# Clustered attention and a gated feed-forward: reordering conversion work and maxima among five queues, and laying the first row shifts by matrix products

## The chip, the cores and the metric

The kernel runs on one core of one Trainium2 chip. The metric is the device time of one execution in microseconds (us). The five engines have queues of their own, and each works through its queue in order: TensorE (PE in the profile; its weight loads are PEld), VectorE (DVE), ScalarE (ACT), GpSimd (POOL) and SyncE (SP), which here only issues transfers.

## The reference

```python
# q, k, v: (4, 8, 768, 64); centroids: (8, 16, 64); w_in: (512, 2048); w_out: (2048, 512)
q_assign = argmax(einsum('bhsd,hcd->bhsc', q_n, c_n), -1)     # rows normalised
k_assign = argmax(einsum('bhsd,hcd->bhsc', k_n, c_n), -1)
mask   = q_assign[:, :, :, None] == k_assign[:, :, None, :]
scores = where(mask, scale * q @ k.T, -1e9)
scores = scores - max(scores, -1)
attn   = exp(scores) / (sum(exp(scores), -1) + 1e-9)
x      = (attn @ v) laid out as (4 * 768, 512)
h      = x @ w_in
out    = (h * erf(log(1 + exp(h)))) @ w_out
```

Each query attends only to the keys of its own cluster, and the attention output goes through a feed-forward with the activation h·erf(softplus(h)). The feed-forward weights arrive in double precision.

## The kernel before, in words

**Pairs and units.** Two heads are worked on together as a pair: four batches of four pairs. A pair has 12 units: two halves of the queries (384 each) times six blocks of 128 keys. A unit `u` has these stages:

- `products`: scores q·k of both heads, in float32 (`sc<-qT,kT` in the profile);
- the rest of `scores`: a bf16 product that adds the mask (`sc<-qm,km`), and on ScalarE the exponential into `pr`;
- `accumulate`: GpSimd adds up the exponentials (`acc`);
- `attend`: the product with v (`av`);
- `divide`, once per half: the denominators (`psum`, `inv`, `den`) and the result into `xT`.

**The mask, the shift and the rows.** The mask is built into the operands `km` and `qm`: their lower rows hold, per cluster, a one-hot code (or minus a large number), so that their product adds a large negative number where the clusters differ. One more row of each head (partition `SH` = 32 for head 0, 96 for head 1) holds in `qm` the negated shift of each query and in `km` ones, so the same product also subtracts it. `route(p)` finds the clusters: it transposes q and k on VectorE, casts them into `qm` and `km` (`vectors`), multiplies with the centroids (`psim`), finds the best (`sims`, `mx`, `hot`, `hotT`), and `choose` picks the first winner by a product (`wonq`, `wonk`) and copies it into the operands. These are the mask copies: four on ScalarE into `km`, two on ScalarE and two on VectorE into `qm`. Pairs of later batches use `choose_later`, which works without `won`.

**The maxima.** `shift(p)` computes the shift: for each of six blocks of queries, two halves of the keys and two heads a product `sm<-km,qm` and, on VectorE, a maximum over 384 (`nmx<-sm`). After three blocks the shifts of one half (`nm`) are complete, and `turn(p, h)` brings them from a column per block into the row: a transposition on TensorE (`pn`), a copy on ScalarE (`nmT`), and six transfers of 128 elements (`qm<-nmT`).

**The weights.** `convert()` turns the double-precision weights into float32 in 32 steps of 128x512 with integer tricks. A step `n` has: two ScalarE operations that split the words (`split`), one VectorE maximum, one ScalarE operation for the signs (`signs`), a transfer for a later step (`fetch`), then, in a second call, a VectorE shift and a GpSimd addition, and the next step's `split`. Every `yield` ends a call; `prepare(n)` makes `n` calls. In the profile all of these have `w_out` or `a_s` as their ScalarE output, since the raw words are staged there.

**The order.** The first batch's attention has its order written out by hand. Two units form a period; a pair has six, counted by `r` = 0, 2, 4, 6, 8, 10. For each, `plan` gives five numbers: how many steps of the pair's own `aside` (routing, then maxima) go ahead of the scores, how many of the next pair's; how many of each go behind them; and how many conversion calls follow. `turn(p, 1)` stands ahead of r=4, `turn(p+1, 0)` ahead of r=10. With `keep_in_program_order` the engines keep the order of the program here; near the end of the batch (`in_order[0] = False`) the scheduler may reorder. From the second batch on, the feed-forward's products (`hp`, `po`) fill the gaps between units, and the rest of the conversion is spread out.

**Buffers.** PSUM has two tiles for scores (`ps_s`) and four for everything else (`ps_x`): `sm`, `psim`, `won`, `pn`, `psum`, `av`, `hp`, `po`. An `av` tile stays in use over a half.

The plan before, one line per three periods, as (own ahead, next ahead, own behind, next behind, conversion calls):

```python
(1, 0, 1, 1, 0), (1, 0, 0, 2, 0), (0, 0, 0, 1, 4),
(0, 1, 0, 2, 2), (0, 1, 0, 2, 0), (0, 1, 0, 2, 2),
```

In the next pair's `aside`, the first call is the transposition and the cast of q, the second `psim` and the cast of k, the third the choice of winners, the fourth the mask copies; each call after that is two maxima.

Of the kernel before, what the change touches and what calls it, by code (L numbers as in the profile page):

```python
# [8 lines left out]
F32 = mybir.dt.float32  # L9
# [9 lines left out]
P = 128  # L19
B, H, S, D = 4, 8, 768, 64  # L20
# [4 lines left out]
HW = S // 2  # L25
HJ = NJ // 2
# [14 lines left out]
SH = 2 * C  # L41
# [27 lines left out]
def kernel(  # L69
# [10 lines left out]
    nc = tc.nc  # L80

    in_order = [True]
    te, ve, ae, ge = (
        InOrder(tc, e, in_order) for e in (nc.tensor, nc.vector, nc.scalar, nc.gpsimd)
    )

    def pool(name, bufs, **kw):
        return ctx.enter_context(tc.tile_pool(name=name, bufs=bufs, **kw))
# [13 lines left out]
    ps_x = pool("ps_x", 4, space=PSUM)  # L102

    ident = const.tile([P, P], F32, name="ident")
    identb = const.tile([P, P], BF16, name="identb")
# [20 lines left out]
    pairs = {}  # L126
# [43 lines left out]
    for base, pattern, sign, op, fill in (  # L170
# [5 lines left out]
            out=first, in_=first, compare_op=op, fill=fill, base=base, pattern=pattern,  # L176
# [9 lines left out]
    w_steps = []  # L186
# [11 lines left out]
        return actp.tile([P, NFT // 2, TB], F32, name="a_s")  # L198

    steps = {}  # L200

    def fetch(done):

        for n in range(max(done + 1, 0), min(done + 5, len(w_steps))):
            at = places[n]
            if n in steps or (at < 4 and at in places[done + 1 : n]) or (at == 4 and n > done + 2):
                continue
            t = half_tile() if at == 4 else w_out[:, 4 * at : 4 * (at + 1)]
            t = t.rearrange("p f t -> p (f t)").bitcast(U32)
            nc.sync.dma_start(out=t[:, 0 : 2 * LC], in_=w_steps[n][1])  # L210
            raw = t[:, 0 : 2 * LC].rearrange("p (n w) -> p n w", w=2)
            steps[n] = raw[:, :, 1], raw[:, :, 0], t[:, 2 * LC : 3 * LC], t[:, 3 * LC : 4 * LC]

    def split(n):

        if n < len(w_steps):
            hi, lo, m, x = steps[n]
            ae.activation(out=x.bitcast(F32), in_=hi.bitcast(F32), func=ACT.Abs, scale=UP)
            ae.activation(out=m.bitcast(I32), in_=lo, func=ACT.Copy, scale=2.0**-29)

    def signs(n):

        hi, _, m, _ = steps[n]

        ae.activation(
            out=m.bitcast(I16)[:, 1 : 2 * LC : 2], in_=hi.bitcast(F32), func=ACT.Prelu,
            scale=2.0**-25, alpha=2.0**90,
        )

    def convert():  # L230

        split(0)
        for n in range(len(w_steps)):
            _, _, m, x = steps[n]
            w = w_steps[n][0]
            xf = x.bitcast(F32)
            ve.tensor_scalar(out=xf, in0=xf, scalar1=2.0, scalar2=None, op0=ALU.max)
            signs(n)

            fetch(n - 2 if n < n_w_in else n - 1)  # L240
            yield
            ve.tensor_scalar(
                out=w.bitcast(U32), in0=x, scalar1=3, scalar2=None, op0=ALU.logical_shift_left
            )

            ge.tensor_tensor(out=w.bitcast(I32), in0=w.bitcast(I32), in1=m.bitcast(I32), op=ALU.add)
            converted[0] = n + 1
            split(n + 1)
            yield

    load_qk(0)
# [18 lines left out]
    for it in range(2):  # L270
# [4 lines left out]
            out=twice, in0=ss, scalar=inv, in1=norm, op0=ALU.mult, op1=ALU.add  # L275
# [3 lines left out]
            out=norm, in0=twice, scalar1=0.5, scalar2=(1e-6 if it else 0.0),  # L279
# [124 lines left out]
    def shift(p):  # L404


        st = pairs[p]
        nmx = maxima[p % 2]
        load(p, "v", v, vp)
        for h in range(2):  # L410
            ts = slice(h * HJ, (h + 1) * HJ)
            for t in range(h * HJ, (h + 1) * HJ):
                for half in range(2):
                    for e in range(2):
                        sm = ps_x.tile([P, HW], F32, name="sm", tag="x")
                        te.matmul(
                            sm, lhsT=st["qm"][:, e, t * P : (t + 1) * P],
                            rhs=st["km"][:, e, half * HW : (half + 1) * HW], start=True, stop=True,
                        )
                        ve.tensor_reduce(  # L420
                            out=nmx[:, e, t, half : half + 1], in_=sm, axis=AX.X, op=ALU.max, negate=True
                        )
                    if (t, half) != ((h + 1) * HJ - 1, 1):
                        yield
            nm = small.tile([P, 2, HJ], BF16, name="nm")
            ve.tensor_reduce(out=nm, in_=nmx[:, :, ts], axis=AX.X, op=ALU.min)
            st["nm", h] = nm
            if p >= HP:
                yield
                turn(p, h)  # L430
            yield

    def turn(p, h):

        st = pairs[p]
        pn = ps_x.tile([2 * HJ, P], BF16, name="pn", tag="x")
        te.transpose(out=pn, in_=st["nm", h].rearrange("p e t -> p (e t)"), identity=identb)
        nmT = small.tile([2 * HJ, P], BF16, name="nmT")
        ae.copy(out=nmT, in_=pn)
        for e in range(2):  # L440
            r = e * D + SH
            for t in range(HJ):

                queue = nc.scalar if (p, h, e) == (0, 0, 1) else nc.sync
                queue.dma_start(
                    out=st["qm"][r : r + 1, e, h * HW + t * P : h * HW + (t + 1) * P],
                    in_=nmT[e * HJ + t : e * HJ + t + 1],
                )

# [7 lines left out]
    def products(u):  # L459
        p, half, j = units[u]  # L460
        st = pairs[p]
        sc = sc_of[u] = ps_s.tile([P, 2, 512], F32, name="sc", tag="s")
        for e in range(2):
            r = slice(e * D, (e + 1) * D)
            te.matmul(
                sc[:, e, 0:HW], lhsT=st["kT"][r, j * P : (j + 1) * P],
                rhs=st["qT"][r, half * HW : (half + 1) * HW], start=True, stop=False,
            )
# [182 lines left out]


    conv = convert()

    def prepare(n):
        for _ in range(n):
            next(conv, None)
# [3 lines left out]
    def aside(p):  # L661
# [3 lines left out]


    plan = (
        (1, 0, 1, 1, 0), (1, 0, 0, 2, 0), (0, 0, 0, 1, 4),
        (0, 1, 0, 2, 2), (0, 1, 0, 2, 0), (0, 1, 0, 2, 2),
    )  # L670
    ready = {0: aside(0)}
    part = iter(())
# [1 line left out]
    def advance(p, n):  # L674
        for _ in range(n):
            next(ready[p])
# [5 lines left out]
    for e in range(2):  # L682
        ve.tensor_copy(
            out=ccT[e * D : (e + 1) * D, :, e * C : (e + 1) * C],
            in_=pct[e * D : (e + 1) * D].rearrange("d (r e c) -> d r e c", e=2, c=C)[:, :, e],
# [11 lines left out]
    for e in range(2):  # L697
        ve.reduce_sum(
            out=own[:, e : e + 1],
            in_=ident.rearrange("p (g x c) -> p x g c", x=2, c=C)[:, e], axis=AX.XY,  # L700
        )
    advance(0, 1)
    products(0)
    products(1)
    advance(0, 2)
    prepare(2)
    advance(0, NJ + 1)
    turn(0, 0)
    prepare(1)
    advance(0, HJ - 1)  # L710
    for slot in range(0, 2 * NJ * HP, 2):
        p, r = divmod(slot, 2 * NJ)
# [4 lines left out]
        if r == 4:  # L717
            turn(p, 1)
        elif r == 10 and p + 1 < HP:
            turn(p + 1, 0)  # L720
# [34 lines left out]
    for u in range(2 * NJ * HP, len(units), 2):  # L755
        p, half, j = units[u]
# [59 lines left out]
```

The softmax here doesn't subtract the row's maximum and nothing guards it: scores larger than these inputs give would overflow.

## Time and profile before

| | |
|---|---|
| time, median of 3 (lowest to highest) | 1215.78 us (1215.23 to 1217.73) |
| span of the profiled run | 1211.9 us |
| TensorE busy | 1150.3 us (95%) |
| VectorE, ScalarE, GpSimd busy | 43%, 47%, 38% |
| mean granted TensorE clock | 0.977 |

The span is the time of the profiled execution on the core. Nearly all lines of the kernel carry the line number L60 in the profile, the helper through which instructions are issued, so groups are told apart by the tiles that they write and read: `sm<-km,qm` is the maxima's product, `nmx<-sm` the maximum itself. A wait is written as the engine that waited, an arrow, and the engine and tile that released it. Busy shares are averages over stages that differ: the first batch's attention takes roughly the first 175 us, and the feed-forward fills the rest.

### The profile page before, as it was taken

The page shows a single profiled execution, that of the slowest core. Times are in us where ns is not written, and L with a number is a line of the kernel's source. Part 1 is how long each engine was busy: PE and PEld are TensorE (multiplying, and loading weights), DVE is VectorE, ACT ScalarE, POOL GpSimd, SP SyncE. Part 2 cuts the span into 40 slices and gives each one's busy share as a digit, 9 for nine tenths or more (in the row PEclk, how much of TensorE's full clock was granted, in tenths as well). Part 3 has the DMA queues.
Part 4 walks back from the last instruction along what each step waited for, and adds up shares of the span by engine and source line. Part 5 has one row for each costly group of instructions (what it writes and reads, how often), then busy time and mean ns, then how long its engine had stood idle before and what let it go on. Part 6 is the DMA issues. An engine that isn't in the chain of part 4 may idle for free.

```text
span 1211.9 us, 13334 instructions
## 1 busy us (share of the span) xinstructions
PE 1150.3 (95%) x4905; PEld 622.7 (51%) x4905; DVE 518.1 (43%) x976; ACT 571.0 (47%) x680; POOL 460.5 (38%) x466
## 2 busy tenths in 40 slices
PE   4888879899999989999999999999999999999998
PEld 1223337554454545465465455556456456576663
DVE  6576783764444444344263345335354112111121
ACT  4676586677343535173454355165264163122222
POOL 2665764555332433144244243344143343031200
PEclk7799889999999999999999999999999999999999
DMA  7543432212020201020200202001000000000000
GB/s 136 126 94 73 84 112 63 86 48 47 2 48 10 48 8 33 9 36 14 36 22 1 48 10 40 9 17 32 10 23 1 10 9 1 18 1 18 1 17 18
DMA packets 140753, 42.95 MB, mean 35 GB/s; under 512 B 133520, under 2 KB 133520, under 8 KB 140688
## 3 DMA queue, kind: packets, MB, share of 16 engines
q1 hardware_dynamic: 137456, 41.70, 15.7%
q10 hardware_dynamic: 3232, 0.39, 0.3%
q8 instruction: 39, 0.64, 0.2%
q14 instruction: 26, 0.21, 0.1%
HBM read 35.68 MB, written 6.29 MB: 35 GB/s over the span
## 4 chain that ended last, share of the span: by engine, by line
PE 79%; DVE 7%; issue 6%; ACT 5%; DMA 2%; POOL 1%; ACTq 0%; SPq 0%; DVEq 0%; POOLq 0%
PE hp L60 25%; PE po L60 25%; PE sc L60 13%; PE av L60 9%; PE sm L60 4%; DVE nmx L60 2%; PE psum L60 1%; PE psim L60 1%; ACT km L60 1%; ACT L60 1%; DVE w_out L60 1%; DVE den L60 1%; DMA a_s<-in_moe_w_out_dram 1%; ACT inv L60 1%; ACT w_out L60 1%
## 5 line engine op out<-in xcount | busy, mean ns | idle before, releaser
L60 PE MATMUL hp<-xT,w_in 128*128 128x256 f32 x1536 | 381.4, 385 | 2.8 <-DVE xT L60 2.0
L60 PE MATMUL po<-w_out,g 128*128 128x512 f32 x768 | 368.0, 597 | 0.6 <-DVE den L60 0.6
L60 PEld LDWEIGHTS hp<-xT,w_in 128*128 128x128 f32 x1536 | 285.9, 191 | 119.9 <-issue 81.0
L60 POOL TENSOR_TENSOR acc<-acc,pr 128x384 f32<-128x384 f32 x256 | 238.2, 961 | 283.4 <-ACT pr L60 283.3
L60 DVE TENSOR_REDUCE nmx<-sm 128x1 f32<-128x384 f32 x384 | 195.7, 551 | 149.6 <-PE sm L60 148.7
L60 ACT ACT_TABLE_LOAD x110 | 141.1, 1283 | 234.6 <-DVE g L60 128.9
L60 ACT ACTIVATE pr<-sc 128x768 f32<-128x768 f32 x192 | 145.0, 806 | 157.2 <-PE sc L60 156.7
L60 PEld LDWEIGHTS po<-w_out,g 128*128 128x128 f32 x768 | 142.2, 190 | 105.9 <-issue 93.0
L60 POOL TENSOR_TENSOR g<-a_s,g 128x512 f32<-128x512 f32 x88 | 110.5, 1287 | 214.7 <-ACT a_s L60 214.7
L60 PE MATMUL sc<-qT,kT 64*128 64x384 f32 x768 | 178.3, 526 | 4.8 <-ACT pr L60 4.7
L60 DVE COPY g<-hp 128x512 f32<-128x512 f32 x96 | 66.0, 687 | 265.8 <-PE hp L60 265.6
L60 PE MATMUL av<-pr,in_v 128*64 128x386 f32 x768 | 141.2, 509 | 0.6 <-DVE nmx L60 0.6
L60 PE MATMUL sm<-km,qm 128*128 128x384 bf16 x384 | 109.8, 347 | 31.0 <-DVE nmx L60 20.2
L60 PEld LDWEIGHTS sc<-qT,kT 64*128 64x128 f32 x768 | 73.8, 192 | 80.5 <-issue 46.7
L60 POOL TENSOR_TENSOR acc<-pr,pr 128x384 f32<-128x384 f32 x64 | 63.5, 1013 | 104.9 <-ACT pr L60 104.9
L60 PEld LDWEIGHTS av<-pr,in_v 128*64 128x64 f32 x768 | 52.2, 140 | 79.5 <-issue 68.8
L60 PEld LDWEIGHTS <-qm 128*128 128x128 bf16 x384 | 35.2, 99 | 105.4 <-issue 80.8
L60 DVE SCALAR_TENSOR_TENSOR den<-psum,inv 128x384 f32<-128x384 f32 x32 | 17.7, 554 | 124.5 <-ACT inv L60 124.1
L60 ACT ACTIVATE a_s<-a_s 128x2048 f32<-128x2048 f32 (+3 forms) x48 | 62.0, 1309 | 15.1 <-DMA a_s<-in_moe_w_out_dram 14.6
L60 ACT ACTIVATE a_s<-g 128x2048 f32<-128x2048 f32 x24 | 45.9, 1910 | 39.2 <-DVE g L60 39.1
L60 PE MATMUL sc<-qm,km 64*128 64x384 bf16 x384 | 56.2, 328 | 4.3 <-DMA qm<-nmT 4.3
L60 ACT ACTIVATE w_out<-w_out 128x512 f32<-128x512 f32 (+2 forms) x72 | 47.0, 702 | 8.9 <-DMA w_out<-in_moe_w_out_dram 4.7
(72 smaller groups left out, 544.4 us busy)
## 6 DMA issues: line engine op xcount, KB each, us to landing
w_out<-in_moe_w_in_dram SPq DMA_DIRECT2D x16, 512.0 KB, 4.5
in_q<-in_q_dram SPq DMA_DIRECT2D x64, 96.0 KB, 3.1
in_v<-in_v_dram SPq DMA_DIRECT2D x32, 192.0 KB, 2.9
out_dram<-osb SPq DMA_DIRECT2D x24, 256.0 KB, 2.0
in_k<-in_k_dram SPq DMA_DIRECT2D x60, 96.0 KB, 3.4
w_out<-in_moe_w_out_dram SPq DMA_DIRECT2D x8, 512.0 KB, 3.7
a_s<-in_moe_w_out_dram SPq DMA_DIRECT2D x8, 512.0 KB, 3.3
qm<-nmT SPq DMA_DIRECT2D x189, 0.2 KB, 1.7
```

Of the source, the lines that this page charges most:

```text
L60: ins = getattr(self.engine, name)(*args, **kw)
```

## The change

The change has three parts. First, the split of step `n+1` is queued in the first call of step `n`, right after `signs(n)`, instead of at the end of its second call; `split(upto)` splits everything up to a step that has been fetched, and remembers in `cut` what it did. The splits of steps 0 and 1 are queued by hand at the start. It is meant to keep VectorE's conversion operations from waiting for splits that stand behind other ScalarE work. Second, the plan moves maxima away from the period whose ScalarE queue holds the mask copies: no maxima ahead of the scores of r=6, four ahead of r=8 and r=0; and it spreads the conversion calls: one each in r=0 and r=2, two instead of four in r=4. Third, the first shifts of all are laid into their row by six products with one column of `nm` each (`turn_first`), whose outputs start at the row's own partition, and by one copy per head, instead of a transposition, a copy and six transfers.

```diff
-    def split(n):
-
-        if n < len(w_steps):
+    def split(upto):
+
+        for n in range(len(cut), upto + 1):
+            if n not in steps:
+                return
+            cut.append(n)
             hi, lo, m, x = steps[n]
             ae.activation(out=x.bitcast(F32), in_=hi.bitcast(F32), func=ACT.Abs, scale=UP)
             ae.activation(out=m.bitcast(I32), in_=lo, func=ACT.Copy, scale=2.0**-29)
...
     def convert():
 
-        split(0)
         for n in range(len(w_steps)):
+            split(n)
...
             signs(n)
+            split(n + 1)
...
             converted[0] = n + 1
-            split(n + 1)
             yield
...
+    def turn_first():
+
+        st = pairs[0]
+        pn = ps_x.tile([P, HJ, P], F32, name="pnr", tag="x")
+        for e in range(2):
+            r = slice(e * D + SH, e * D + SH + 1)
+            for t in range(HJ):
+                te.matmul(pn[r, t], lhsT=st["nm", 0][:, e, t : t + 1], rhs=identb, start=True, stop=True)
+            (ae.copy, ve.tensor_copy)[e](
+                out=st["qm"][r, e, 0:HW], in_=pn[r].rearrange("p t n -> p (t n)")
+            )
...
     plan = (
-        (1, 0, 1, 1, 0), (1, 0, 0, 2, 0), (0, 0, 0, 1, 4),
-        (0, 1, 0, 2, 2), (0, 1, 0, 2, 0), (0, 1, 0, 2, 2),
+        (2, 0, 0, 1, 1), (1, 0, 0, 2, 1), (0, 0, 0, 1, 2),
+        (0, 0, 0, 2, 2), (0, 2, 0, 2, 0), (0, 1, 0, 2, 2),
     )
...
     advance(0, 1)
+    split(0)
     products(0)
     products(1)
     advance(0, 2)
+    split(1)
     prepare(2)
     advance(0, NJ + 1)
-    turn(0, 0)
+    turn_first()
     prepare(1)
```

More of the change, by code (lines that the diff above doesn't have):

```diff
@@ L200 @@
     steps = {}
+    cut = []
     def fetch(done):
@@ L442, in turn @@
             for t in range(HJ):
-                queue = nc.scalar if (p, h, e) == (0, 0, 1) else nc.sync
-                queue.dma_start(
+                nc.sync.dma_start(
                     out=st["qm"][r : r + 1, e, h * HW + t * P : h * HW + (t + 1) * P],
```

## The prediction

> **What bounds the kernel now.** I read the page first, then the table by windows, the chain that ended last, and the timeline of one pair of heads.
>
> ```profile
> span 1211.9 us, 13334 instructions
> ...
> PE   4888879899999989999999999999999999999998
> ...
> PEclk7799889999999999999999999999999999999999
> ```
> The page: TensorE is busy nearly throughout, except in the first six slices of 30.3 us, where its clock is also low.
>
> ```profile
> 60.00:90.00 30.00, 25.09 (x138) 9.08 (x134) 22.51 (x42) 23.52 (x36) 18.06 (x19) 0.93 0.42 92
> ...
> 120.00:150.00 30.00, 25.85 (x134) 8.91 (x130) 21.24 (x42) 17.51 (x28) 20.78 (x22) 0.89 0.35 78
> ...
> 300.00:400.00 100.00, 99.21 (x426) 48.06 (x430) 43.78 (x87) 37.91 (x51) 35.18 (x39) 1.00 0.13 26
> ```
> The windows (busy time of PE, PEld, DVE, ACT, POOL, then clock): from 300 us TensorE is 99% busy at full clock, so a microsecond won early is kept. In the first batch's attention (30 to 175 us) it idles 4 to 5 us in 30, and no other engine is full either. That is a queue waiting on a queue, and the chain shows which:
>
> ```profile
> 115.15 0.81 ACT pr L60
> ...
> 115.98 0.57 ACT km L60
> ...
> 118.93 0.57 ACT qm L60
> ...
> 119.53 1.25 ACT w_out L60 x2
> ...
> 120.80 1.29 ACT w_out L60 x2
> ...
> 122.11 1.10 DVE w_out L60
> 123.21 0.48 DVE nmx L60
> ...
> 123.73 1.41 PE sm L60 x3
> 125.14 2.77 PE av L60 x8
> ```
> Read from top: exponential, six mask copies, conversion splits, a conversion op on VectorE, a maximum, and only then TensorE. It stands in each of the first three pairs at the same place, period r=4 to r=6; TensorE does little from 79.2 to 86.3 us in the second pair. Then it pays again:
>
> ```profile
> 84.00:85.00 1.00, 0.00 (x0) 0.00 (x0) 0.35 (x1) 1.00 (x3) 0.81 (x1) 1.00 0.00 0
> ...
> 86.00:87.00 1.00, 0.73 (x2) 0.21 (x2) 1.00 (x3) 0.99 (x2) 1.00 (x2) 0.50 0.78 295
> ...
> 91.00:92.00 1.00, 1.00 (x5) 0.57 (x6) 0.95 (x2) 0.00 (x0) 1.00 (x2) 0.50 0.71 262
> ...
> 93.00:94.00 1.00, 1.00 (x10) 0.30 (x6) 0.00 (x0) 0.44 (x1) 0.00 (x0) 1.00 0.00 0
> ```
> The clock (third figure from the end) is halved for some 6.8 us after the gap; a period's av products take 2.77 us there against 1.45 elsewhere in the chain.
>
> At the start, the same chain, earlier:
>
> ```profile
> 25.88 0.18 DVE nm L60
> ...
> 29.10 1.66 DMA qm<-nmT
> ...
> 30.90 0.83 PE sc L60 x4
> ```
> The first shifts are known at 26.06 and reach the scores at 30.90, through a transposition, a copy and six small transfers.
>
> **What the Trainium skill says.** (1) "TensorE: Matmul & The Clock Gate", What's actually happening: the clock halves after an idle window of about 3.4 us and comes back after a busy one; the windows run freely. The trace agrees on the grid (drops at about 44.8 and 85.8 us are twelve windows apart) but a window need not be empty: the one ending at 44.8 was 1.6 of 3.4 us busy. (2) "DMA: Bandwidth & Descriptors", Anatomy of one DMA: about 2.0 us fixed, mostly the write's receipt (stated for another issuing path); the qm<-nmT transfers here have 1.7 us median. (3) The TensorE page, What picks the tile position: a product's output may start at partition 0, 32, 64 or 96. That is what lets the shifts land in rows 32 and 96; no product of the kernel before has a one-row output.
>
> **The change, part by part.** I call S the start of a period's score products on TensorE. In the second pair S is 66.05, 70.17, 75.16, 81.17, 91.13, 98.57, 103.50 for r = 0, 2, 4, 6, 8, 10 and the next 0: lengths 4.12, 4.99, 6.01, 9.96, 7.44, 4.93, together 37.45 us. The same work at full clock is about 28 us (six periods of 1.81 sc + 1.45 av; 24 maxima products at 0.215; psum 1.6, psim 0.8, won and pn 0.6).
>
> *a. First shifts by products, first split earlier.* ScalarE waits 2.19 us for wonk before its mask copies; the first split (2 x 0.67 = 1.33) fits there and costs nothing. Then VectorE's first conversion op need not wait until 19.39: it follows the qm copies at 16.4, its two ops end at 17.3, and the twelve maxima, 0.48 each, end at 23.1 instead of 25.86: 2.7 us. The shifts: six products of 128 columns (between 0.1 and 0.27 each, the pn product being 0.27; I take 0.2, so 1.2) and two copies of 1x384. Unknown: at least the 0.25 of the nmT copy, at most the 0.57 of a 384-column copy; I take 0.5, side by side on two engines. About 1.8 us replaces 4.84. The rows are thus ready near 25. But the program now puts eight maxima products ahead of the first scores (six before), and VectorE needs 0.48 for each: scores near 27.9 instead of 30.9. **3.0 us**, with two maxima already done that formerly came after.
>
> *b. Splits a period sooner.* Nothing is removed: each conversion step keeps three ScalarE ops (2.05 to 2.08 together), two VectorE (0.43 each) and one GpSimd (1.27). Only the order changes. In r=4, VectorE's conversion op finds its split done in r=2, so no split behind the mask copies holds the maxima queue: the 2.58 + 1.10 us of conversion in the chain above leave it.
>
> *c. Two of r=4's four conversion calls go to r=0 and r=2.* r=0 gets VectorE 0.43 and GpSimd 1.27, hidden: VectorE waits for sm there. r=2 gets ScalarE 2.05 and VectorE 0.43. That isn't hidden: ScalarE's r=2 is 1.51 (pr) + 1.12 (inv) + 1.67 (km cast) + 0.25 (nmT) = 4.55 of 4.99. The conversion is queued ahead of nmT, so in r=4 nmT ends 2.1 later, at S4+3.45, and pr starts at S4+3.5 instead of S4+1.82. Behind nmT stand six transfers whose rows the r=6 scores read: at 0.61 per issue (76.55, 3.66 for six) plus 1.7 the last lands at S4+8.25; at the 6.1 us of the fourth pair (151.34 to 157.42), at S4+9.5. This is the change's new wait: TensorE has nothing from about S4+5.8 until then, bar one score in between.
>
> *d. Maxima away from the mask copies.* r=6 no longer begins with two maxima that wait for km; its scores' first products go at S4+4.4 instead of S4+6.0. The eight maxima of r=6 and of r=8's head then run at VectorE's pace.
>
> Sum from S4 to S8: ScalarE: pr to 5.0, km copies 7.4, qm 8.5, conversion 10.6, r=6's pr 12.1. TensorE: scores' masks end at 8.7 to 9.6, four maxima 1, av 1.45, four maxima 1.9 (VectorE: 4 x 0.49, 0.86 of conversion, 4 x 0.49): S8 = S4+12.8 to 13.7 at full clock. The new gap is long enough to halve the clock where the window falls badly; then av takes 2.8 and maxima 0.47 each: S8 = S4+16.0. I take S4+14.5, against 15.97: -1.5. r=8 then runs at full clock, about 6.9 for 7.44: -0.5. The four maxima ahead of r=0 cost +0.7 there and give 0.4 back: +0.3. **-1.7 a pair, three pairs -5.1.** The fourth pair has a routing of its own; its km copies now come behind r=6's pr, which waits for the same transfers, but six ScalarE ops fewer stand before them: **0**, from -1 to +2.
>
> *e. Afterwards* the order of work is the same and TensorE the bound: carried over in full.
>
> Sum: 3.0 + 5.1 = 8.1: **1207.7 us**.
>
> **The rivals.**
> - *All gain, no new gap*: the transfers land early and the clock holds: S8 at S4+12.8: 3.2 + 0.6 - 0.3 = 3.5 a pair, 10.5 + 3.0: 1202.3. For: TensorE's floor of 28 us leaves room for nine. Against: ScalarE's overfull r=2.
> - *The new wait takes the old one's place*: the shift transfers and a halved clock give S8 at S4+16: 0.2 a pair, 0.6 + 3.0: 1212.2. For: 1.6 us busy in a window was already too little. Against: with six issues at 0.61 the gap is only 2.4.
> - *Given back later*: the second batch's start hangs on the remaining conversions (waits on a_s transfers of 3.15 to 3.35 us near 227 to 249 us), half of 8.1 lost: 1211.7. For: those waits are on the chain. Against: they are relative, started by the work before.
> - *Slower*: r=2's 2.05 us lie on the path in full in all four pairs, 8.2 against the start's 3.0: 1221. For: ScalarE is in order, pr and nmT are behind it. Against: 3.7 us of conversion leave the chain in the same pair.
>
> **How the numbers follow.** Forecast 0.45, no new gap 0.20, new wait 0.22, given back 0.07, slower 0.06. The range 1202.0 to 1212.8 takes in the first four. The bound of 0.2% lies at 1213.3: the forecast and the full gain are faster, of the two cases near 1212 about two thirds: 0.85. Same 0.09, slower 0.06.
>
> **What would show it.** In the trace after: first scores near 28 us (a); no conversion between qm copies and maxima in the chain (b); nmT of r=4 behind three w_out ops, and a wait of sc on qm<-nmT in r=6 of each pair (c); r=4 to r=8 near 14.5 us (d); equal lengths after 300 us (e). Wrong would be: no such wait on the transfers (then it's nearer 1202), a pair of 37 us or more, or a first score after 29.5.

## The result and the profile after

| | before | after |
|---|---|---|
| median, first measurement | 1216.6 us (4 runs, 1215.23 to 1217.73) | 1201.19 us (4 runs, 1197.01 to 1205.72) |
| profiled execution, span | 1211.9 us | 1204.0 us |
| TensorE busy | 1150.3 us | 1148.0 us |

The ratio is 0.9875, with a 95% interval of 0.9837 to 0.9912: faster by about 15 us. The four times after spread over 8.7 us, the four before over 2.5; in later measurements of 11 or 12 runs, the kernel before spread over 4.6, 7.0 and 8.4 us, so a wide spread is not peculiar to the changed kernel. The profiled execution is the slowest of the four, so the two traces differ by 7.9 us only.

The page after, rows as before the change:

```profile
span 1204.0 us, 13336 instructions
...
PE   4888899899999989999999999999999999999998
...
PEclk8899999999999999999999999999999999999999
```

and the windows, with the same columns as in the prediction (busy PE, PEld, DVE, ACT, POOL, clock):

```profile
60.00:90.00 30.00, 25.70 (x147) 9.51 (x146) 21.72 (x45) 24.09 (x38) 23.53 (x24) 1.00 0.46 111
...
120.00:150.00 30.00, 24.73 (x144) 9.14 (x141) 24.27 (x46) 18.76 (x29) 19.28 (x20) 0.98 0.30 56
...
300.00:400.00 100.00, 99.43 (x438) 48.05 (x437) 43.25 (x85) 42.31 (x55) 29.96 (x32) 1.00 0.15 29
```

TensorE is hardly busier than before in the same 30 us, but its clock is 1.00 and 0.98 there where it was 0.93 and 0.89, and the work comes earlier. What stands at the old place now shows in the chain that ended last (start, length, what), in the third pair:

```profile
106.42 0.56 ACT w_out L60
...
107.60 0.66 ACT w_out L60
108.26 0.14 ACT nmT L60
108.45 0.32 PE wonk L60
...
110.21 1.34 PE sc L60 x7
111.55 1.68 DMA qm<-nmT
...
113.36 0.48 PE sc L60 x3
...
115.14 2.77 PE av L60 x8
```

The splits behind the mask copies, and the maximum behind the splits, are gone from this chain. In their place stand conversion, the copy nmT behind it, the transfers behind that, and the scores behind the transfers. The second product of r=4, wonk, waits for nmT too, by 1.1 us. In this pair the clock falls again (av at 2.77 us). The second pair has the same chain and keeps its clock:

```profile
77.87 1.59 DMA qm<-nmT
...
79.60 0.48 PE sc L60 x3
...
81.32 1.45 PE av L60 x8
```

The start after:

```profile
23.93 0.18 DVE nm L60
...
24.16 0.34 PE pnr L60 x3
24.52 0.48 ACT qm L60
...
25.04 0.34 PE pnr L60 x3
...
25.48 0.56 DVE qm L60
...
29.01 0.77 PE sc L60 x4
```

Eleven further runs were made. The table gives their medians and, from each trace, the time from S4 to S8 in the second and third pair (S: start of a period's first score products), and the start of ScalarE's first activation over a whole half tile (`a_s<-g`), the first gate, a mark at the end of the first batch. The runs were made on several chips; each ratio is to runs of the kernel before on the same chip, whose medians lie between 1214.2 and 1216.6 us.

| kernel | median us | ratio to before, 95% | S4 to S8 | first gate |
|---|---|---|---|---|
| before | 1216.6 | 1 | 15.97, 15.97 | 191.2 |
| after | 1201.19 | 0.9875 (0.9837 to 0.9912) | 12.44, 14.05 | 179.7 |
| e1_after | 1204.21 | 0.9904 (0.9882 to 0.9927) | 13.98, 12.52 | 180.2 |
| e11_after | 1202.62 | 0.9895 (0.9872 to 0.9918) | 12.44, 12.51 | 179.5 |
| e2_start | 1209.93 | 0.9962 (0.9948 to 0.9976) | 15.97, 15.99 | 188.1 |
| e3_no_start | 1204.91 | 0.9910 (0.9893 to 0.9926) | 12.35, 14.05 | 181.8 |
| e4_split_only | 1207.67 | 0.9943 (0.9924 to 0.9963) | 12.91, 12.92 | 182.7 |
| e5_plan_only | 1208.08 | 0.9945 (0.9925 to 0.9966) | 13.66, 13.86 | 181.2 |
| e8_warm | 1202.73 | 0.9899 (0.9884 to 0.9915) | 12.44, 12.53 | 177.6 |
| e6_turn_first | 1198.20 | 0.9862 (0.9843 to 0.9880) | 11.13, 11.13 | 174.3 |
| e7_r8 | 1196.70 | 0.9850 (0.9831 to 0.9869) | 11.24, 11.31 | 171.9 |
| e9_early | 1197.38 | 0.9852 (0.9826 to 0.9878) | 11.24, 11.23 | 173.5 |
| e10_prod | 1203.59 | 0.9906 (0.9886 to 0.9925) | 11.23, 11.23 | 178.8 |

The changed kernel's first four runs were probably a favourable draw: the two later medians, of six runs each, are 1204.21 and 1202.62, though the three intervals overlap. In all three of its traces the first gate comes 11.1 to 11.8 us sooner than in the trace before; that is the part that repeats.

### The profile page after: what moved, and what is told of

The parts are those of the page before. It is cut to its first block, busy times and chain, and to the rows that moved or that the text cites. A ratio compares the mean times of both kernels' runs of the same rounds, so it can differ in the third digit from the quotient of the medians.

```text
span 1204.0 us, 13336 instructions
## 1 busy us (share of the span) xinstructions
PE 1148.0 (95%) x4910; PEld 621.8 (52%) x4910; DVE 513.9 (43%) x977; ACT 569.7 (47%) x680; POOL 461.0 (38%) x466
## 4 chain that ended last, share of the span: by engine, by line
PE 79%; issue 7%; DVE 5%; ACT 4%; DMA 4%; POOL 1%; SPq 0%; ACTq 0%; DVEq 0%; POOLq 0%
PE hp L60 26%; PE po L60 25%; PE sc L60 13%; PE av L60 8%; PE sm L60 4%; DVE nmx L60 2%; PE psum L60 1%; PE psim L60 1%; ACT L60 1%; DMA a_s<-in_moe_w_out_dram 1%; DMA in_k<-in_k_dram 1%; DMA w_out<-in_moe_w_out_dram 1%; DVE den L60 1%; ACT inv L60 1%; DMA qm<-nmT 1%
## 5 line engine op out<-in xcount | busy, mean ns | idle before, releaser
L60 PE MATMUL sm<-km,qm 128*128 128x384 bf16 x384 | 105.8, 341 | 19.5 <-DVE nmx L60 13.0
L60 ACT COPY nmT<-pn 6x128 bf16<-6x128 bf16 x31 | 7.7, 248 | 87.6 <-PE pn L60 87.6
```

The costliest lines, as they stand in the source:

```text
L60: ins = getattr(self.engine, name)(*args, **kw)
```

## The experiments

**e1_after and e8_warm: what spreads the times.** e1_after is the changed kernel unaltered. e8_warm puts eight products whose result nobody reads where TensorE waits for the transfers:

```diff
+        if us[0] < 2 * NJ * HP and us[0] % (2 * NJ) == NJ:
+            idle = ps_x.tile([P, HW], F32, name="idle", tag="x")
+            for _ in range(8):
+                te.matmul(idle, lhsT=identb, rhs=pairs[units[us[0]][0]]["km"][:, 0, 0:HW], start=True, stop=True)
```

> The changed kernel once more, for other draws of its time and another trace. Theory 'clock': the change leaves two short waits of TensorE around r=4 and r=6 (about 1.1 us on won, 1.5 us on the shift transfers), and the free-running activity window decides whether they halve the clock; so the times spread over 1195 to 1206, each follows its own granted clock (about 1.2 us for each 0.001), and the median is 1198 to 1202. Rival 'queues': the order of the queues alone sets the time; the spread has to come from the later batches and does not follow the clock, and S4 to S8 is the same in every trace (12.4 us in the second pair, 14.0 in the third).

> The changed kernel with eight extra products of 128x384 that nobody reads, between the first products of r=6 and its mask products, where TensorE waits for the shift transfers; about 1.7 us of work in a wait of 1.5. Theory 'clock': the clock stays at 1.00 through r=6 and r=8 of all pairs, S4 to S8 is 12.4 to 12.8 us in the second and the third pair alike, the spread narrows and the median falls to 1195 to 1199. Rival 'queues': the extra products stand ahead of the mask products in an in-order queue and cost up to 0.3 us a pair: 1200 to 1204, with the same spread.

In e1_after it is the second pair that loses its clock and the third that keeps it, the other way round than in the first trace. The second pair in the first trace, then in e1_after (the clock is the third figure from the end):

```profile
80.00:85.00 5.00, 4.35 (x23) 1.79 (x24) 4.55 (x10) 4.81 (x8) 4.12 (x5) 1.00 0.99 275
80.00:85.00 5.00, 4.62 (x17) 1.43 (x18) 2.62 (x6) 4.95 (x9) 4.13 (x5) 0.66 0.95 262
```

The program is the same, so the order of the queues alone does not decide between 12.4 and 14.0 us. The traces show what goes with it. The shortest stretches at half clock last 3.4 us. The two falls in the first trace, at 43.2 and 114.9 us, lie 21 times 3.41 us apart. If time is cut into windows of 3.41 us, counted from the first fall after 40 us, every change of the clock up to about 165 us falls on an edge of a window, in the trace before and in all three of the changed kernel. A window at full clock in which TensorE was busy for 1.70 us or less was followed by half clock every time (twelve cases), one with 1.85 us or more never. In the first trace of the changed kernel, the windows with the wait for the transfers and those after them are, for the second and for the third pair:

```profile
77.35:80.77 3.42, 1.91 (x13) 0.59 (x10) 0.38 (x1) 3.35 (x6) 3.42 (x4) 1.00 0.29 65
80.77:84.18 3.41, 2.86 (x15) 1.04 (x16) 3.34 (x9) 3.39 (x7) 2.53 (x4) 1.00 1.01 284
...
111.49:114.90 3.41, 1.58 (x10) 0.47 (x8) 0.75 (x2) 3.33 (x7) 3.41 (x5) 1.00 0.47 106
114.90:118.31 3.41, 3.41 (x11) 1.06 (x11) 1.87 (x5) 3.38 (x6) 2.47 (x3) 0.50 0.88 300
```

The waits for the transfers are alike (1.42 and 1.50 us), but in the third pair a wait of 0.32 us for the maxima falls into the same window, and in the second pair most of it comes after the edge. The edges lie differently in each execution: the first fall comes at 43.2, 43.9 and 44.6 us in the three traces of the changed kernel. In the first pair the clock fell in all three, and S4 to S8 took 14.3 to 14.5 us. This was read from the traces afterwards; no experiment moved the edges.

e8_warm, with the wait filled, kept the clock at 1.00 through its first three pairs, as theory 'clock' said, but not in the fourth: S4 to S8 took 12.2 us in the first pair, 12.44 and 12.53 in the next two, and its first gate came 2.6 us before e1_after's. Nothing of this reached the end: its median of 1202.73 lies in the rival's range, and its ratio overlaps that of e1_after, whose own median of 1204.21 lies outside the 1198 to 1202 of theory 'clock'. From 200 us, e8_warm's windows show where the lead goes:

```profile
200.00:205.00 5.00, 2.40 (x13) 1.10 (x15) 2.23 (x4) 4.94 (x5) 1.56 (x2) 0.91 0.00 0
205.00:210.00 5.00, 5.00 (x16) 2.49 (x9) 4.29 (x8) 3.51 (x6) 5.00 (x5) 0.50 0.08 13
210.00:215.00 5.00, 5.00 (x13) 3.30 (x12) 2.48 (x5) 2.01 (x3) 2.21 (x2) 0.57 0.35 116
```

and e1_after's the same place:

```profile
200.00:205.00 5.00, 4.05 (x22) 2.24 (x21) 0.82 (x2) 4.94 (x5) 0.00 (x0) 1.00 0.35 79
205.00:210.00 5.00, 3.27 (x14) 1.49 (x14) 3.48 (x6) 4.97 (x7) 3.98 (x4) 0.77 0.02 3
210.00:215.00 5.00, 5.00 (x20) 3.39 (x19) 5.00 (x10) 1.40 (x3) 3.77 (x4) 0.89 0.35 105
```

There TensorE waits while ScalarE is full (4.94 of 5 us) with the gates and table loads. In these 15 us it is idle about as long in both (2.6 and 2.7 us), but e8_warm then runs at half clock for some 10.2 us, worked out from the clock in its windows, and e1_after for 3.4. Its third gate activation starts at 246.5 us, e1_after's at 246.2: the whole lead is lost. Later the clock also separates the first trace of the changed kernel from e1_after. Up to the fifth activation they agree (393.36 and 393.40 us); the sixth starts at 448.21 in the first and 445.06 in e1_after. The slower one's windows between:

```profile
400.00:410.00 10.00, 8.89 (x35) 4.76 (x34) 5.25 (x9) 6.66 (x8) 6.67 (x6) 0.92 0.09 31
410.00:420.00 10.00, 10.00 (x42) 6.04 (x43) 5.05 (x10) 2.18 (x4) 5.68 (x7) 0.91 0.01 3
...
430.00:440.00 10.00, 7.33 (x32) 3.72 (x30) 0.69 (x1) 5.07 (x6) 3.59 (x4) 0.83 0.00 0
```

e1_after has 1.00 in all three, with TensorE busy for the same time to within 0.1 us: 3.2 us for the clock alone, and this is all of the difference between the two spans (1204.0 and 1200.8). One more part of the expectation fell: the mean granted clock does not order the runs (0.989 went with 1200.8 and with 1204.7). Only these differences between traces are shown; that the whole spread of 9 us comes from the clock is not, and the kernel before spreads nearly as far on one chip.

**e2_start and e3_no_start: the start alone, and all but the start.** e2 adds `turn_first` and the early `split(0)` to the kernel before; e3 takes both (and `split(1)`) from the changed kernel. Of e3's edit, the lines for the first shifts:

```diff
-    turn_first()
+    turn(0, 0)
```

> Part a alone on the kernel before: the first shifts by products, and the first split queued ahead of the first mask copies. If the start's gain is kept to the end, 2.5 to 4 us less than before (1212.5 to 1214). Rival: the first pair's loads and the conversions set its pace anyway, and the earlier scores wait in r=2 instead: within 1 us of before.

> Everything but part a: the splits a period sooner and the new plan, with the old start (transposition, copy, six transfers). If the parts add up, it is slower than the changed kernel by what e2_start wins, 2.5 to 4 us: 1202 to 1206. Rival: the start wins nothing, and this one is at the changed kernel's time, 1199 to 1202.

Alone, the start's part makes the first gate 3.1 us earlier. The ratio 0.9962 is a gain of 4.6 us, more than the 2.5 to 4 expected, though its interval (2.9 to 6.3) reaches into them. Taken from the changed kernel, the part costs 1.6 to 2.3 us at the first gate, and at the end nothing that these intervals can tell from zero. At the gate the two parts, 3.1 and 9.4 us, come to 12.5 where the whole gains 11.1 to 11.8, so they very nearly add there; at the end the intervals are too wide to say.

**e4_split_only and e5_plan_only: which part opens the queue.** e4 is e3 with the old plan, e5 the kernel before with the new plan, both with the old start.

> The splits a period sooner alone: old plan, old start. In the old plan two conversion calls of the same kind follow each other in r=4, so ScalarE's queue in r=4 to r=6 keeps its order, mask copies, then six splits and signs; only the start and the last pair differ. Theory 'both are needed' (the earlier split has an effect only where the plan leaves a period between two first calls): within 2 us of before, S4 to S8 still 15.9 to 16.0 us. Rival 'the split is what counts': at least half of the changed kernel's gain, 1209 or less, with S4 to S8 below 14.

> The new plan alone: maxima away from r=6's head, conversion calls spread over r=0 and r=2, but each split at the end of the second call as before, and the old start. With the new plan the second calls are in r=0, r=4, r=6 and r=10, so a split in r=4 stands behind the mask copies and a VectorE operation of the same period waits for it. Theory 'both are needed': VectorE's queue still stops in r=4 behind the mask copies, though TensorE no longer depends on it at the head of r=6; S4 to S8 between 13 and 15 us, 1207 to 1212. Rival 'the plan is what counts': S4 to S8 at 12.4 to 14.0 and the time of the kernel without the start's part, 1203 to 1206.

Of e4's two theories the rival was right: the split alone takes S4 to S8 from 15.97 to 12.9 and the time to 0.9943. The names of the tiles hid why. ScalarE's queue still shows six `w_out` operations behind the mask copies, but they are other ones: signs 2, split 3, signs 3, split 4 instead of split 2, signs 2, split 3, signs 3 (numbered as in the first pair). So VectorE's first conversion maximum of the period waits for none of them, and its next one for the second of the six instead of the fourth. The timeline of e4, second pair (start, length, engine, operation, and in brackets the idle time before it and what ended it):

```profile
80.87 3.73 ACT L60 ACTIVATE w_out<-w_out 128x512 int16<-128x512 f32 x6
...
82.19 1.09 DVE L60 TENSOR_SCALAR w_out<-w_out 128x512 f32<-128x512 f32 x1 [1.47 <-ACT w_out L60]
...
83.20 2.87 DVE L60 TENSOR_REDUCE nmx<-sm 128x1 f32<-128x384 f32 x6
83.80 1.25 PE L60 MATMUL sm<-km,qm 128*128 128x384 bf16 x3 [1.68 <-DVE nmx L60]
```

The maxima still stand behind a conversion that waits for ScalarE, but TensorE waits 1.68 us instead of 2.95 (the wait that ends at 86.27 us in the trace before), and the av products that follow take 1.52 us: the clock stays up. e5 came out as its first theory said: 13.7 to 13.9, the maxima behind a VectorE operation that stands behind a split, and r=6 at 9.3 to 9.5 us. By the ratios each alone is worth about 7 us. At the first gate the split gains 8.5 us, the plan 10.0, and the two together, in e3, only 9.4: two remedies for one gap.

**e6_turn_first and e7_r8: the new wait.** e6 moves `turn(p, 1)` from the head of r=4 to r=2, ahead of that period's conversion call. e7 moves the conversion call itself to r=8:

```diff
-        (2, 0, 0, 1, 1), (1, 0, 0, 2, 1), (0, 0, 0, 1, 2),
-        (0, 0, 0, 2, 2), (0, 2, 0, 2, 0), (0, 1, 0, 2, 2),
+        (2, 0, 0, 1, 1), (1, 0, 0, 2, 0), (0, 0, 0, 1, 2),
+        (0, 0, 0, 2, 2), (0, 2, 0, 2, 1), (0, 1, 0, 2, 2),
```

> The changed kernel with the shifts of a pair's second half laid in r=2, ahead of that period's conversion call instead of behind it: the nmT copy stands before the three w_out operations in ScalarE's queue. If the wait for the six transfers is what remains in r=6 (1.4 to 1.6 us of TensorE per pair), it falls under 0.3 us, S4 to S8 comes to 10.8 to 11.6 us in the second and third pair, and the first product of the gates' first tile starts 4 to 8 us sooner; the time 1195 to 1200. Rival: the exponentials and mask copies, still behind the conversion, take over: S4 to S8 stays above 12.

> The changed kernel with the conversion call of r=2 in r=8 instead: ScalarE's r=2 is then as in the kernel before (4.6 us in a period of 5.0), and r=8, where it had about 2.6 us of work in 6.8, takes the 1.9 us. If ScalarE's overfull r=2 is what delays the exponentials, mask copies and transfers of r=4, S4 to S8 comes to 10.5 to 11.5 us, r=8 stays at 6.8 to 7.0, and the time is 1195 to 1200. Rival: the call only moves the wait to r=8 and r=10, which get longer by what r=4 to r=8 wins; 1200 to 1204.

Both expectations of the first theory held, but for one figure: in e6 TensorE still waits 0.36 us for the transfers in the second pair, and up to 0.7 elsewhere, where less than 0.3 was expected. In e7, nmT is early again and the scores' wait is down to 0.98 us:

```profile
70.31 0.25 ACT L60 COPY nmT<-pn 6x128 bf16<-6x128 bf16 x1
...
70.59 3.67 SPq L447 DMA_DIRECT2D qm<-nmT  x6
...
75.44 0.48 PE L60 MATMUL sc<-qm,km 64*128 64x384 bf16 x3 [0.98 <-DMA qm<-nmT]
```

S4 to S8 is 11.2 to 11.3 us, r=8 is 6.83 as in the changed kernel, and all five runs lie within 2.4 us (1195.04 to 1197.44). In the second pair what was won lies in r=4, 3.54 us instead of 4.97, where wonk no longer waits for nmT; r=6 is no shorter (7.70 for 7.47), since the product of its last maximum now waits 0.99 us for VectorE. In the first pair the clock stays at 1.00, and S4 to S8 is 12.0 us where the changed kernel had 14.3 to 14.5. e6 saves the same 1.4 us in r=4 and loses 0.6 in r=2 (5.62 for 4.99). e7_r8 is faster than the changed kernel in its two later measurements: its interval, up to 0.9869, lies below those of e1_after and e11_after, from 0.9882 and 0.9872. It overlaps that of the first measurement, and e7_r8 was not run on one chip with e1_after or e11_after.

**e9_early, e10_prod and e11_after: what is left.** e9 is e7 with the copy nmT ahead of the km cast of r=2; e10 is e7 with products in the place of all transfers of the first batch; e11 is the changed kernel on the same chip.

> e7_r8 with the second half's shifts laid as soon as they are known: their copy stands ahead of the km cast of r=2, about 1.7 us sooner. In e7_r8 the mask products of r=6 still waited 1.0 us for the last transfers. If that wait is on the path, S4 to S8 falls from 11.2 us to 10.2 to 10.6, and the time to 1193 to 1196. Rival: VectorE's eight maxima and the exponentials of r=6 behind the mask copies set S8 anyway: S4 to S8 stays at 11 or above and the time within 1 us of e7_r8 (1195.7 to 1197.7).

> e7_r8 with all shifts of the first batch laid by six products and two copies, none by transfers. No wait of sc on qm<-nmT is left. The copies cost ScalarE 0.48 instead of 0.25 us and VectorE 0.56 us more at r=4 and r=10. If transfers are the remaining limit of r=6: S4 to S8 10.2 to 10.6, 1193 to 1196. Rival: the copy on VectorE stands behind the routing and the denominators of r=2 and r=4, so the second head's row comes as late as by transfer, and the six products fill TensorE: 1196 to 1199.

> The changed kernel a third time, on one chip with the two above. Theory 'clock': median 1200 to 1205, spread of more than 6 us, above both. Rival: the difference from e7_r8 was one of chips, and it lies within 2 us of them.

e9's rival was right: without the wait on the transfers S4 to S8 stays at 11.2, while r=2 gets 0.65 us longer. So in e7_r8 the transfers are no longer the limit there. e11_after, at 1202.62 with a spread of 7.9 us, came as theory 'clock' said, except that it lies above e9_early only and not above e10_prod (1203.59). e10 was slower than e7_r8, by another way than either theory said. In the waits of TensorE (total, times, longest):

```profile
PE pnr L60 <- ACT qm L60: 7.9, 8, 1.6
```

The second head's three products start only when ScalarE has copied the first head's row, although they go to another partition. Why was not tried. The period r=2, at whose end they stand, takes 7.00 us instead of 4.99.

## Why the prediction was right and wrong

The direction, the mechanism and the new wait were right; the time was too long. The measured 1201.19 lies 0.8 us below the range, whose lower end was 1202.0, and the two later medians, 1204.21 and 1202.62, lie inside it; that the first fell outside may be the draw of its four runs. What repeats is the gain at the first gate: 11.5 us on average over the three traces, where the sum had 8.1. The step that failed is d.

*a, the start.* Forecast: nm ready at 23.3, rows near 25, scores near 27.9. Measured in the first trace: 24.1, 26.0 and 29.0. Three things were not in the sum: the loads landed 0.35 us later; the first score products ran 2.93 us instead of 2.39, so that wonq behind them started another 0.3 us late; and the second three of the six products waited from 24.49 to 25.04 us. By the first pair's S8 the gain was 3.1 to 4.4 us in three traces; the forecast had 3.0 + 1.5.

*b, the splits.* As described; but the sum credited it jointly with the rest, and e4 and e5 show that either the splits or the plan alone gives most of the gain at the first gate.

*c, the new wait.* The forecast put nmT's end at S4+3.45, the last landing at S4+8.25 and r=4's pr at S4+3.5; in the second pair they are at S4+3.2, S4+8.1 and S4+3.1. e6 and e7 show that the late nmT was on the path: with it early, the first gate comes 5 to 8 us sooner. A wait that was missed is wonk's, 1.1 us: the trace names nmT as its releaser, wonk starts 0.05 us after nmT ends, and in e7_r8, where nmT is done earlier, it does not wait. The reason, perhaps a PSUM tile that nmT sets free, was not tried.

*d, the failed step.* S8 was taken as S4+14.5 in every pair, between 12.8 at full clock and 16.0 at half. In the first pair, where the clock fell in all three traces, it was 14.3 to 14.5. In the second and third it was 12.44 to 12.52 (four times, clock kept) and 13.98 to 14.05 (twice, clock lost): 13.0 on average. The full-clock end was nearly right, though its own terms (masks to 8.7 or 9.6, then 1.0, 1.45 and 1.9) give 13.05 to 13.95 and not 12.8 to 13.7. The half-clock end was 1.5 to 2 us too dear, and it was given about half the weight where it came twice in six. It charged eight maxima and the av products at half clock, for the 6.8 us taken from the trace before, behind masks that end near S4+9.4. In the first pair the clock was low for all of 6.8 us in the first trace, and S8 was still S4+14.4: the masks ended at S4+8.6, and a maxima product took 0.39 us instead of 0.47. In the later pairs the low clock cost even less, as the windows of the third pair show:

```profile
112.00:114.00 2.00, 0.64 (x5) 0.29 (x6) 0.00 (x0) 1.94 (x4) 2.00 (x4) 1.00 0.33 73
114.00:116.00 2.00, 1.68 (x8) 0.68 (x8) 1.85 (x4) 1.98 (x5) 1.64 (x2) 0.73 0.97 220
116.00:118.00 2.00, 2.00 (x7) 0.37 (x5) 0.77 (x3) 2.00 (x5) 1.42 (x2) 0.50 0.91 360
118.00:120.00 2.00, 1.73 (x9) 0.75 (x9) 1.62 (x4) 0.48 (x1) 1.82 (x2) 0.92 0.17 68
```

The first three of r=6's four maxima products were done before the clock fell and the fourth took 0.37 us; little but av ran at half, and the clock was back after 3.4 us. So the second and the third pair gained about 3.2 us each on average (2.1 to 3.7, from S8 to S8), where 1.7 was forecast; r=8 (6.83), r=10 (5.74 for 4.93) and r=0 (3.70 for 4.12) came out as worked out. The fourth pair was put at 0: it gained 0.9 in two traces and lost 1.3 in the third (e11, r=6 at 14.44 us, 3.45 of them a wait for the transfers), and the stretch from its S8 to the first gate gained another 1.3 each time, which the forecast had not looked at. So from the 8.1 forecast to the 11.5 measured it is -0.8 up to the first pair's S8, +2.9 in the second and third pair, and +1.3 at the end.

*e, afterwards.* The 11 us at the first gate are about what the later medians show at the end. The first measurement's further 3 to 4 us were not repeated by the two later ones. That they come from the clock is not shown: only the slowest of its four executions was traced.

Of the rivals, "all gain, no new gap" (1202.3) was nearest in time, but not in cause: the gap that it denied is there in every trace. "Given back later" was wrong for the change itself (the third gate activation keeps 11 us), and right for e8_warm, whose lead went at half clock between 205 and 215 us.

## What to carry to other kernels

Before moving work to an earlier period, add up the engine's queue there: ScalarE's r=2 was full, and what was pushed aside was the start of a chain of transfers. The same call in r=8, where ScalarE had room, was worth 3 to 7 us more by the ratios. Two remedies for one gap don't add (8.5 and 10.0 us at the first gate, 9.4 together), so price them together; and where order is compared by tile names, check which step an operation belongs to.

## What was not expected of the hardware

The same program has 12.4 or 14.0 us at one place, in different pairs of different executions. In four traces, from 40 to 165 us, the clock changed only at the edges of windows of 3.41 us, whose place differs from one execution to the next, and it was the busy time within a window, not the length of one wait, that went with a fall: up to 1.70 us of 3.41 busy at full clock was followed by half clock, from 1.85 us on it was not. After a fall the clock was back after 3.4, 6.8 or 10.2 us, one to three windows (3.4 us in the third pair of the first trace after; 10.2, from 44.6 to 54.8 us, in the trace before, where waits lay in between). How busy a window must be for that is open: one that was 90% busy brought the clock back (e11_after, 44.6 to 48.0 us), one that was 93% busy did not (e1_after, 43.9 to 47.3 us). With a wait filled by products that nobody reads, the clock held in three pairs of four, the first among them, where it fell in all three traces without them; but this brought nothing once the work ran into the next wait.
